# A new order of steps and engines from batch 6's attention on, and two operands' places swapped

## The chip, the cores and the metric

The kernel runs on one core of a Trainium2 chip. The metric is the device time of one execution in microseconds (us). Five engines work side by side, each through its own instructions in order: TensorE (PE, matrix products), VectorE (DVE), ScalarE (ACT), GpSimd (POOL), and SyncE (SP), which starts DMA transfers. They wait for one another through semaphores.

## What is computed

Attention of 8 batches with 8 heads and 576 queries of width 64, whose keys and values are means of 8 neighbours (72 of each), and then a two-layer network over the 4608 resulting tokens of width 512:

```python
k_p = k.reshape(B, H, Sp, pool, D).mean(axis=3)
v_p = v.reshape(B, H, Sp, pool, D).mean(axis=3)
scores = scale * np.matmul(q, k_p.transpose(0, 1, 3, 2))
scores = scores - np.max(scores, axis=-1, keepdims=True)
attn = np.exp(scores)
attn = attn / (np.sum(attn, axis=-1, keepdims=True) + 1e-09)
x = np.matmul(attn, v_p) ...          # (4608, 512)
h = x @ w_in                           # (512, 2048)
g = h * (1.0 / (1.0 + np.exp(-1.702 * h)))
out = g @ w_out                        # (2048, 512)
```

All is fp32. A product of two fp32 operands is made on PE from their high and low parts: each operand is split by a cast (the high part, on ACT or DVE) and a difference (the low part, on POOL or DVE), and three products are summed in a PSUM bank. That is why one entry of a product shows as three or six matmuls.

## The kernel before

The batches are worked one after the other. While PE computes the network of batch c, the other engines and a part of PE prepare the attention of batch c + 1. The last stage handles 1024 tokens at once: the 512 of batch 7 and 8 x 64 that the earlier batches left over.

The width 2048 is cut into 8 pairs p of 256. In the products with w_in a scheme of seven products in place of eight (as Strassen's, in Winograd's form) is used: operands "11" and "21" are quarters of x itself, "22", "t1", "t2", "t3" and "t4" are the last quarter and sums of quarters. For batch 6 these operands lie in `x6` and `xs6_2`, `xs6_3`, ..., its products with w_in go to the banks ha6_p and hb6_p (L1882), and its products with w_out to o6_0, o6_128, o6_256 and o6_384 (L2086 to L2088, three matmuls per pair of parts, here called an o-triple). What ACT and DVE make of a bank before an o-triple is ghall and glall, the high and low part of the gelu, in buffers of the rings `gh` and `gl`.

The 1024-token stage has these steps:

- The late operands: `late_split` and `late_combine` (L1508 to L1548) make y11, y21, y22, yt1 to yt4 from the quarters xtl. `late_op` (L1478) says where they lie; three of them take places of batch 6's operands, so they can be written only when batch 6's last product has read there.
- `hidden(p)` (L2136): seven products of six 512-column matmuls: "11", s2, s3 and "22" into the bank la_p, "12" into lb_p, s1 and s4 into lc_p (L2154). ACT or DVE copies the bank away (`keep`, L2166), DVE adds the other bank (`plus`, L2171), ACT applies the gelu (L2179). A later product into la_p waits for the copy.
- `fold_out(p)` (L2210): sums of w_out's pair, u (L2221, L2232), split into tf (L2237, L2240) in buffers of the rings `gh`, `gl` and `osb`, and written to memory (td, L2253). `fetch_sums` reads them back (ta, tb).
- `operands(th, p)` (L2297): for either half th of the tokens, the operands oa, ob, oc, od with the sums ou, out of the gelus (L2322, L2325, L2331). `outgoing` (L2364): seven products m1 to m7 per pair and half, 112 of six 256-column matmuls (L2376). `combined(th)` adds their banks up (L2404, L2409) and writes the rows out.

Each step is a task of a plan with an engine. The order is written out: `ORDER` is a text of 4738 tokens such as `P:la7_0#0`, whose letter is the engine (A ACT, V DVE, G POOL, P PE, D a DMA on SP's queue, O a writing of rows), and a star moves the task to its other engine: a copy from ACT to DVE, a sum or difference from POOL to DVE. Every engine executes its own tasks in this order, so a task that waits holds all that stands behind it on its engine.

Of the kernel before, what the change touches and what calls it, by code (L numbers as in the profile page):

```python
# [372 lines left out]
A:at7_0#0 A:at7_0#1 V:qt7_1#2 P:ha6_3#1 P:o6_256#5 *A:cs6_3#1 P:o6_128#4 V:nm7_1#0 V:nm7_1#1 A:gh6_3#0 P:o6_128#5
A:cs6_3#2 V:sc7_1#0 P:o6_384#4 G:gl6_3#0 V:qt7_1#3 P:ha6_3#2 V:sc7_1#1 D:ws6_5#1 V:at7_0#0 P:sps7_1#1 A:cs6_3#3
V:cs6_3#1 V:at7_0#1 P:o6_0#6 A:gh6_3#2 V:mt7_0#0 A:cs6_3#6 P:ha6_3#3 *A:ah7_0#0 V:nm7_1#2 G:gl6_3#2 D:ws6_5#3
P:hb6_3#2 V:al7_0#0 A:cs6_3#4 A:gh6_3#1 V:mt7_0#1 P:hb6_4#0 D:ws6_5#2 A:cs6_3#5 V:cs6_3#2 P:hb6_4#1 A:ah7_0#1
V:sc7_1#2 G:gl6_3#1 P:ha6_4#0 V:nm7_1#3 V:al7_0#1 D:ws6_6#0 P:pav7_0#0 V:sc7_1#3 P:o6_384#5 A:xtl0_0#0 *A:cs6_4#0
P:pav7_0#1 A:sc7_1#0 V:mt7_0#2 P:o6_0#7 V:cs6_4#0 *A:ah7_0#2 P:ha6_4#1 V:al7_0#2 A:xtl0_0#1 V:mt7_0#3 P:o6_256#6
A:y1_0#0 V:sm7_1#0 G:xtl0_0#0 A:cs6_4#1 P:o6_128#6 A:gh6_3#3 P:o6_384#6 A:gh6_4#0 A:cs6_3#7 G:xtl0_1#0 P:ha6_4#2
*A:y1_1#0 A:cs6_4#2 V:y1_0#0 A:ah7_0#3 D:ws6_6#1 V:y1_1#0 P:pav7_0#2 A:yt1_0#0 G:gl6_3#3 *A:cs6_4#3 P:o6_128#7  # L380
A:y1_0#1 V:cs6_4#1 G:gl6_4#0 P:ha6_4#3 A:xtl0_0#2 V:al7_0#3 A:gh6_4#2 V:sm7_1#1 G:yt1_0#0 D:ws6_6#3 P:o6_256#7
A:cs6_4#6 V:y1_0#1 A:cs6_4#4 P:hb6_4#2 G:gl6_4#2 A:gh6_4#1 A:cs6_4#5 D:ws6_6#2 P:pav7_0#3 V:cs6_4#2 P:o6_0#8
# [15 lines left out]
P:ha6_7#2 A:gh6_6#1 G:yt3_1#0 *A:yt3_1#1 *G:yt3_0#1 A:cs6_6#5 D:ws7_1#1 P:o6_384#11 *A:cs6_7#3 G:yt3_1#1 A:gh6_6#3
P:o6_128#12 A:cs6_6#7 G:gl6_6#1 P:ha6_7#3 A:gh6_7#0 *G:gl6_6#3 A:cs6_7#2 D:ws7_1#3 P:o6_256#12 *A:y2_0#0 A:y2_0#1
*G:gl6_7#0 A:cs6_7#4 P:o6_0#13 G:y2_0#0 P:o6_384#12 G:y2_0#1 V:cs6_7#1 P:o6_128#13 A:gh6_7#1 P:la7_0#0 A:cs6_7#5  # L400
A:gh6_7#2 *G:gl6_7#1 A:cs6_7#6 P:o6_256#13 *G:gl6_7#2 P:lb7_0#0 D:ws7_2#0 P:o6_384#13 P:o6_0#14 P:hb6_7#2 D:ws7_1#2
A:y2_1#0 *A:y2_1#1 P:lc7_0#0 V:cs6_7#2 G:y2_1#1 *G:y2_1#0 A:gh6_7#3 *G:xtl1_1#1 P:o6_0#15 G:xtl0_2#0 A:cs6_7#7
P:la7_1#0 A:osb6_0#0 *A:yt2_0#1 *A:yt2_1#1 G:xtl0_0#1 *G:xtl1_0#1 A:yt2_0#0 P:o6_256#14 O:osb6_0#0 *A:yt2_1#0
*G:yt2_0#1 A:yt4_0#1 P:o6_128#14 G:yt2_0#0 *G:yt2_1#0 A:yt4_1#1 *G:yt2_1#1 A:yt4_0#0 P:o6_384#14 G:gl6_7#3
*A:yt4_1#0 *G:yt4_0#1 G:yt4_0#0 *G:yt4_1#0 A:store0_0#0 P:o6_256#15 *G:yt4_1#1 G:u1_0#0 A:store1_0#0 *G:u1_1#0
P:o6_128#15 A:osb6_256#0 V:store0_0#0 P:la7_0#1 G:u0#0 A:osb6_128#0 O:osb6_256#0 *G:u0#1 P:lb7_1#0 *A:store0_1#0
A:store0_0#1 G:u0#2 O:osb6_128#0 *A:tf0_0#0 D:ws7_3#0 P:la7_0#2 G:u0#3 V:store1_0#0 A:tf0_2#0 G:tf0_1#0 *G:tf0_2#0
A:w#33 P:la7_1#1 D:ws7_2#1 A:store1_0#1 *A:store0_1#1 G:w#33 V:store0_1#0 P:la7_0#3 G:u1_2#0 A:store1_1#0 *G:u1_3#0
D:td0_0#0 A:store0_1#2 D:td0_0#1 P:lc7_0#1 *G:u1#0 A:store0_0#2 D:ws7_2#3 A:store0_0#3 *G:u1#1 D:td0_1#0 P:lc7_1#0
A:ob0_0#0 V:store0_1#1 G:u1#2 A:tf1_0#0 D:ws7_2#2 *G:ob0_0#0 G:u1#3 A:store0_1#3 P:o6_384#15 *A:tf1_2#0 *G:tf1_1#0  # L410
G:tf1_2#0 P:la7_1#2 A:w#34 D:td1_0#0 A:osb6_384#0 *G:w#34 D:td1_0#1 *G:u1_4#0 G:u1_5#0 P:la7_2#0 D:ws7_3#1
A:store1_1#1 O:osb6_384#0 *G:u2#0 V:store1_1#0 P:lb7_2#0 G:u2#1 A:store2_0#0 D:td1_1#0 A:store1_1#2 *G:u2#2
D:ws7_4#0 P:la7_1#3 *A:tf2_0#0 A:tf2_2#0 G:u2#3 V:store2_0#0 G:tf2_1#0 *G:tf2_2#0 P:lc7_1#1 A:w#35 D:ws7_3#3
*A:store1_0#2 A:store2_0#1 D:td2_0#0 *G:w#35 A:store1_0#3 P:la7_2#1 *G:u1_6#0 G:u1_7#0 D:ws7_3#2 V:store1_1#1
P:lc7_2#0 G:u3#0 A:store2_1#0 D:td2_0#1 *G:u3#1 A:store1_1#3 D:td2_1#0 P:la7_2#2 *A:tf3_0#0 G:u3#2 D:td3_0#0
*G:tf3_1#0 G:u3#3 A:tf3_2#0 P:la7_3#0 *A:store2_1#1 D:ws7_4#1 G:tf3_2#0 A:w#36 V:store2_1#0 P:lb7_3#0 G:w#36
A:store3_0#0 D:td3_0#1 *G:u1_8#0 G:u1_9#0 A:store2_1#2 D:td3_1#0 P:la7_2#3 V:store3_0#0 D:ws7_5#0 G:u4#0
# [2072 lines left out]
```

## Time and profile before

| | us |
|---|---|
| median of three runs | 902.42 |
| lowest and highest run | 901.66 and 902.71 |
| profiled execution | 900.38 |
| its span | 898.6 |

The profiled execution is one of its own, 2.04 us below the median; 1.8 us of it lie outside the span. Times of rows count from the span's start. Busy times of PE come from pipelined matmuls whose ends are modelled, so a start-to-start distance tells more than a length.

### The profile page before, as it was taken

To read this page: it belongs to the slowest core of one execution; us is meant where nothing else is said; L and a number is where in the kernel's file an instruction comes from. 1 tells how busy PE (TensorE), PEld (TensorE's weight loads), DVE (VectorE), ACT (ScalarE), POOL (GpSimd) and SP (SyncE) were. 2 spreads that over 40 slices of the span, in tenths; PEclk is the share of its full clock that TensorE was granted. 3 is DMA by queue.
4 is the path that set the end of the run, shared out by engine and by line. 5 is a ranking of instruction groups with operands and counts; after the bars stand their busy time and mean duration, and the time that the engine had idled before them with its cause. 6 is when DMAs were issued, how large, how long until landed. Compare 5 with 4: busy or idle time off the path is not lost.

```text
span 898.6 us, 15882 instructions
## 1 busy us (share of the span) xinstructions
PE 874.0 (97%) x5404; PEld 780.6 (87%) x5404; DVE 716.8 (80%) x1342; ACT 541.5 (60%) x1188; POOL 387.1 (43%) x377
## 2 busy tenths in 40 slices
...
DMA packets 145793, 174.33 MB, mean 194 GB/s; under 512 B 85169, under 2 KB 96433, under 8 KB 145713
## 3 DMA queue, kind: packets, MB, share of 16 engines
...
## 4 chain that ended last, share of the span: by engine, by line
PE 82%; DVE 4%; POOL 3%; issue 3%; ACT 3%; SPq 2%; DMA 2%; DVEq 0%; POOLq 0%; ACTq 0%
PE ha L1882 13%; PE hb L1882 10%; PE m L2376 9%; PE o L2086 8%; PE o L2087 8%; PE o L2088 8%; PE sps L1128 4%; PE h L1677 3%; PE h L1678 3%; PE h L1679 3%; PE o L1719 2%; PE o L1720 2%; PE o L1721 2%; PE la L2154 2%; POOL u L2221 1%
## 5 line engine op out<-in xcount | busy, mean ns | idle before, releaser
L1936 POOL TENSOR_TENSOR glall<-shared,ghall 128x256 fp32r<-128x256 f32 x80 | 62.8, 790 | 187.5 <-ACT shared L1929 138.9
L2086 PE MATMUL o<-w,ghall 128*128 128x512 f32 x320 | 126.9, 397 | 0.0
L2087 PE MATMUL o<-w,ghall 128*128 128x512 f32 x320 | 126.1, 394 | 0.0
L2088 PE MATMUL o<-w,glall 128*128 128x512 f32 x320 | 125.0, 391 | 0.7 <-POOL glall L1936 0.7
L2088 PEld LDWEIGHTS o<-w,glall 128*128 128x128 f32 x320 | 60.1, 188 | 14.6 <-POOL glall L1936 1.1
L1936 POOL TENSOR_TENSOR glall<-gall,ghall 128x256 fp32r<-128x256 f32 x45 | 34.9, 779 | 87.6 <-ACT gall L1929 51.5
L1882 PE MATMUL ha<-xs,ws 128*128 128x256 f32 x480 | 70.9, 283 | 0.0
L1882 PEld LDWEIGHTS ha<-xs,ws 128*128 128x128 f32 x480 | 66.0, 190 | 4.9 <-ACT shared L1897 0.8
L1882 PE MATMUL hb<-x,ws 128*128 128x256 f32 x480 | 67.2, 283 | 0.0
L2086 PEld LDWEIGHTS o<-w,ghall 128*128 128x128 f32 x320 | 60.6, 189 | 6.2
L1921 ACT ACTIVATE ghall<-shared 128x256 fp32r<-128x256 f32 x108 | 43.9, 415 | 36.6 <-PE o L2087 16.2
L1882 PEld LDWEIGHTS hb<-x,ws 128*128 128x128 f32 x480 | 63.4, 190 | 2.7 <-DVE shared L1904 0.2
L2087 PEld LDWEIGHTS o<-w,ghall 128*128 128x128 f32 x320 | 60.7, 190 | 5.6
L1677 PE MATMUL h<-x,w 128*128 128x256 f32 (+1 forms) x192 | 63.2, 329 | 1.4 <-ACT gh L1699 1.0
L1678 PE MATMUL h<-x,w 128*128 128x256 f32 (+1 forms) x192 | 61.1, 318 | 0.0
L1679 PE MATMUL h<-x,w 128*128 128x256 f32 (+1 forms) x192 | 61.1, 318 | 0.0
L1707 POOL TENSOR_TENSOR gl<-g,gh 128x512 fp32r<-128x512 f32 x28 | 40.0, 1427 | 47.6 <-ACT gh L1699 34.9
L1904 DVE TENSOR_TENSOR shared<-shared,hb 128x256 f32<-128x256 f32 x81 | 33.5, 415 | 22.6 <-PE hb L1882 18.0
L1243 ACT COPY main<-sc 32x256 f32<-32x256 f32 (+2 forms) x109 | 48.5, 445 | 2.9 <-DVE sc L1200 1.1
L1128 PE MATMUL sps<-k,qt 128*128 128x144 f32 x320 | 45.9, 287 | 1.7 <-ACT k L1035 0.7
L1128 PEld LDWEIGHTS sps<-k,qt 128*128 128x128 f32 x320 | 42.7, 190 | 4.1 <-ACT k L1035 1.1
L1929 ACT ACTIVATE shared<-shared 128x256 f32<-128x256 f32 x108 | 43.4, 414 | 3.6 <-ACT osb L1658 0.9
...
## 6 DMA issues: line engine op xcount, KB each, us to landing
...
```

The lines of the kernel that those rows point to most:

```text
L1128: nc.tensor.matmul(ps()[:, t * PW : (t + 1) * PW], lhsT=qt()[:, s0 : s0 + P], rhs=m.k2()[:, jj], start=True, stop=True,)
L1243: copy(out=main()[32 * r : 32 * (r + 1), :, cols].rearrange("p j t (k a) -> p t j a k", a=2), in_=sc()[rows, ts, :, 16 * r : 16 * (r + 1)] ...
L1677: nc.tensor.matmul(o, lhsT=w[:, 0, j], rhs=xs[:, 0], start=j == 0, stop=False)
L1678: nc.tensor.matmul(o, lhsT=w[:, 1, j], rhs=xs[:, 0], start=False, stop=False)
L1679: nc.tensor.matmul(o, lhsT=w[:, 0, j], rhs=xs[:, 1], start=False, stop=j == NJ - 1)
L1882: nc.tensor.matmul(o, lhsT=wv()[:, r, jj], rhs=xo(k, jj), start=start and n == 0, stop=n == len(terms) - 1,  skip_group_check=not start,)
L1921: lambda: nc.scalar.activation(out=gh(), in_=src(), func=AF.Gelu_apprx_sigmoid),
L1936: engine.tensor_tensor(out=gl(), in0=part(i), in1=gh().bitcast(F32), op=ALU.subtract)
L2086: nc.tensor.matmul(o(), lhsT=gh()[:, tok], rhs=w()[:, 0], start=start, stop=False)
L2087: nc.tensor.matmul(o(), lhsT=gh()[:, tok], rhs=w()[:, 1], start=False, stop=False)
L2088: nc.tensor.matmul(o(), lhsT=gl()[:, tok], rhs=w()[:, 0], start=False, stop=stop)
L2376: nc.tensor.matmul(bank()[:, i], lhsT=av(r)[:, i * P : (i + 1) * P], rhs=tv(k), start=p == 0 and i == n == 0, stop=p == NPAIR - 1 and n == ...
```

## The change

`ORDER` is the same up to token 3722. The 1016 tokens behind it, from batch 6's attention part to the end, are the same steps in another order, some of them with the star set or taken away. Of the 1024-token stage, the products lb7_1, la7_0, la7_1 and lb7_0, which take "11" and "21", come first, between o-triples of batch 6; la7_2 and lb7_3 stand with the next ones. Two lines of it, and the two edits beside it:

```diff
-*G:gl6_7#0 A:cs6_7#4 P:o6_0#13 G:y2_0#0 P:o6_384#12 G:y2_0#1 V:cs6_7#1 P:o6_128#13 A:gh6_7#1 P:la7_0#0 A:cs6_7#5
...
+*G:xtl1_1#1 A:gh6_7#3 P:la7_1#0 D:ws7_1#2 A:cs6_7#7 *G:yt2_1#0 A:yt4_0#0 G:yt4_1#0 *G:yt1_1#1 A:yt2_1#1 A:yt3_0#1
...
-            for i, (n, k) in zip(X_PLACES[0], (("t4", 1), ("22", 1), ("t3", 1))):
+            for i, (n, k) in zip(X_PLACES[0], (("22", 1), ("t4", 1), ("t3", 1))):
                 late_ops[n, k] = home(2 * i, [P, 2, CHUNK], F32R, f"y{n}_{k}")
...
-        ha = buf(ps_h, [P, CHUNK], F32, "h", f"la{p}")
-        hb = buf(ps_a, [P, CHUNK], F32, "a", f"lb{p}")
+        ahead = p == 2
+        ha = buf(ps_o if ahead else ps_h, [P, CHUNK], F32, "o" if ahead else "h", f"la{p}")
+        hb = buf(ps_o if ahead else ps_a, [P, CHUNK], F32, "o" if ahead else "a", f"lb{p}")
```

`X_PLACES[0]` is (2, 3, 4). Batch 6 has xs6_2 in place 2 and xs6_3 in place 3; so y22_1 goes from xs6_3's place to xs6_2's, and yt4_1 the other way. The banks la7_2 and lb7_2 come out of the group of banks that held batch 6's o.

The engines of the steps, counted over the whole program (the line numbers are of before, those of after are one lower up to `hidden`):

| steps | DVE | POOL | ACT |
|---|---|---|---|
| late splits and sums (L1516, L1523), before | 18 | 10 | 12 |
| after | 17 | 4 | 19 |
| fold (L2221 to L2240), before | 41 | 38 | 17 |
| after | 40 | 38 | 18 |
| outgoing operands (L2322, L2325, L2331), before | 93 | 42 | 57 |
| after | 112 | 26 | 54 |
| closing sums (L2409), before and after | 14 | 0 | 0 |

PE at the end of batch 6, before: the product hb6_7 that reads xs6_3, between o-triples and the first products of the late stage (la0 and so on are la7_0).

```order
L2086 MATMUL o6_0_7645<-w1_14_1529,ghall0_2959 128x512
L2087 MATMUL o6_0_7645<-w1_14_1529,ghall0_2959 128x512
L2088 MATMUL o6_0_7645<-w1_14_1529,glall0_2977 128x512
L1882 MATMUL hb6_7_8535<-xs6_3_7427,ws6_7_2_8368 128x256 x6
L2154 MATMUL lc0_8661<-yt1_0_8180,ws7_0_1_8423 128x512 x3
L2154 MATMUL lc0_8661<-yt1_1_8491,ws7_0_1_8423 128x512 x3
L2086 MATMUL o6_0_7645<-w1_15_1593,ghall0_2959 128x512
L2087 MATMUL o6_0_7645<-w1_15_1593,ghall0_2959 128x512
L2088 MATMUL o6_0_7645<-w1_15_1593,glall0_2977 128x512
L2154 MATMUL la1_8678<-y11_0_8144,ws7_1_0_8546 128x512 x3
L2154 MATMUL la1_8678<-y11_1_8166,ws7_1_0_8546 128x512 x3
```

After:

```order
L2154 MATMUL lb1_8595<-y21_0_8261,ws7_1_0_8579 128x512 x3
L2154 MATMUL lb1_8595<-y21_1_8331,ws7_1_0_8579 128x512 x3
L2085 MATMUL o6_384_7746<-w1_13_1366,ghall1_3010 128x512
L2086 MATMUL o6_384_7746<-w1_13_1366,ghall1_3010 128x512
L2087 MATMUL o6_384_7746<-w1_13_1366,glall1_3093 128x512
L1881 MATMUL hb6_7_8516<-xs6_3_7427,ws6_7_2_8297 128x256 x6
L2085 MATMUL o6_256_7716<-w1_13_1366,ghall1_3010 128x512
L2086 MATMUL o6_256_7716<-w1_13_1366,ghall1_3010 128x512
L2087 MATMUL o6_256_7716<-w1_13_1366,glall1_3093 128x512
L2085 MATMUL o6_128_7733<-w1_13_1366,ghall0_2959 128x512
L2086 MATMUL o6_128_7733<-w1_13_1366,ghall0_2959 128x512
L2087 MATMUL o6_128_7733<-w1_13_1366,glall0_2977 128x512
```

The product on xs6_3 stands 17 rows earlier, behind a first product lb1 and ahead of la0; the last product that reads xs6_2, whose place y22_1 now takes, stands 24 rows ahead of it.

PE at the last reading of ghall1 and glall1, before:

```order
L2154 MATMUL la0_8620<-yt4_0_8700,shared8_2728 128x512 x3
L2154 MATMUL la0_8620<-yt4_1_8707,shared8_2728 128x512 x3
L2154 MATMUL lc0_8661<-y22_0_8602,ws7_0_2_8509 128x512 x3
L2154 MATMUL lc0_8661<-y22_1_8658,ws7_0_2_8509 128x512 x3
L2154 MATMUL lc1_8820<-yt1_0_8180,ws7_1_1_8576 128x512 x3
L2154 MATMUL lc1_8820<-yt1_1_8491,ws7_1_1_8576 128x512 x3
L2086 MATMUL o6_384_7746<-w1_14_1529,ghall1_3010 128x512
L2087 MATMUL o6_384_7746<-w1_14_1529,ghall1_3010 128x512
L2088 MATMUL o6_384_7746<-w1_14_1529,glall1_3093 128x512
L2154 MATMUL la1_8678<-yt3_0_8554,ws7_1_1_8576 128x512 x3
L2154 MATMUL la1_8678<-yt3_1_8556,ws7_1_1_8576 128x512 x3
```

After:

```order
L2085 MATMUL o6_384_7746<-w1_14_1529,ghall1_3010 128x512
L2086 MATMUL o6_384_7746<-w1_14_1529,ghall1_3010 128x512
L2087 MATMUL o6_384_7746<-w1_14_1529,glall1_3093 128x512
L2154 MATMUL la1_8658<-yt3_0_8541,ws7_1_1_8691 128x512 x3
L2154 MATMUL la1_8658<-yt3_1_8501,ws7_1_1_8691 128x512 x3
L2085 MATMUL o6_256_7716<-w1_14_1529,ghall1_3010 128x512
L2086 MATMUL o6_256_7716<-w1_14_1529,ghall1_3010 128x512
L2087 MATMUL o6_256_7716<-w1_14_1529,glall1_3093 128x512
L2154 MATMUL lc0_8752<-y22_0_8577,ws7_0_2_8571 128x512 x3
L2154 MATMUL lc0_8752<-y22_1_8543,ws7_0_2_8571 128x512 x3
L2154 MATMUL la0_8639<-yt4_0_8669,shared8_2728 128x512 x3
L2154 MATMUL la0_8639<-yt4_1_8628,shared8_2728 128x512 x3
```

POOL at the first fold, whose tf0_1 takes the buffer of ghall1, before:

```order
L1523 TENSOR_TENSOR yt2_0_8688<-xtl0_2_7958,yt2_0_8688 128x256
L1936 TENSOR_TENSOR glall1_3093<-shared12_2925,ghall1_3010 128x256
L1523 TENSOR_TENSOR yt4_0_8700<-xtl0_0_8113,yt4_0_8700 128x256
L2221 TENSOR_TENSOR u0_8730<-w1_0_363 128x512
L2232 TENSOR_TENSOR u0_8730<-u0_8730 128x256 x3
L2240 TENSOR_TENSOR tf0_1_8778<-u0_8730,tf0_0_8764 128x512
L2240 TENSOR_TENSOR w1_0_363<-u0_8730,w1_0_363 128x256
L2221 TENSOR_TENSOR u1_8800<-w1_2_526 128x512
```

After:

```order
L1458 TENSOR_TENSOR xtl0_0_8156<-xtl0_0_8156,xtl0_2_8200 128x512
L1522 TENSOR_TENSOR yt4_1_8628<-xtl0_0_8156,yt4_1_8628 128x256
L1522 TENSOR_TENSOR yt2_1_8651<-xtl1_1_7908,yt2_1_8651 128x256
L2232 TENSOR_TENSOR u0_8702<-u0_8702 128x256 x3
L2240 TENSOR_TENSOR tf0_1_8773<-u0_8702,tf0_0_8771 128x512
L2232 TENSOR_TENSOR u0_8702<-u0_8702 128x256
L2232 TENSOR_TENSOR u1_8793<-u1_8793 128x256 x3
L2240 TENSOR_TENSOR tf1_1_8843<-u1_8793,tf1_0_8819 128x512
L2240 TENSOR_TENSOR w1_2_526<-u1_8793,w1_2_526 128x256
```

The last reading of ghall1 stands behind nine products of the late stage in place of eleven. On POOL tf0_1 is still the first low part, but w1_0's difference is no longer behind it, and one sum of the next pair follows.

DVE at the end, the closing sums of the second half, before:

```order
L2409 TENSOR_TENSOR store0_1_8760<-store0_1_8760,m6_1_9989 128x512
L2409 TENSOR_TENSOR store1_1_8802<-store0_1_8760,m7_1_9978 128x512
L2409 TENSOR_TENSOR store0_1_8760<-store0_1_8760,m5_1_9967 128x512
L2409 TENSOR_TENSOR store3_1_9035<-store1_1_8802,m5_1_9967 128x2x256
L2409 TENSOR_TENSOR store3_1_9035<-store1_1_8802,m4_1_9955 128x2x256
L2409 TENSOR_TENSOR store2_1_8937<-store0_1_8760,m3_1_9997 128x2x256
L2409 TENSOR_TENSOR store2_1_8937<-store0_1_8760,m2_1_9944 128x2x256
```

After:

```order
L2409 TENSOR_TENSOR store2_1_8909<-store0_1_8733,m2_1_9906 128x2x256
L2409 TENSOR_TENSOR store0_1_8733<-store0_1_8733,m6_1_9961 128x512
L2409 TENSOR_TENSOR store1_1_8766<-store0_1_8733,m7_1_9971 128x512
L2409 TENSOR_TENSOR store3_1_8956<-store1_1_8766,m4_1_10004 128x2x256
L2409 TENSOR_TENSOR store3_1_8956<-store1_1_8766,m5_1_9946 128x2x256
L2409 TENSOR_TENSOR store0_1_8733<-store0_1_8733,m5_1_9946 128x512
L2409 TENSOR_TENSOR store2_1_8909<-store0_1_8733,m3_1_9996 128x2x256
```

PE's last five products are m7, m5, m4, m3, m2 before, and m7, m4, m5, m3, m3 after. Before, the sum of m2 is the last and that of m3 the one ahead; now the sum of m2 stands first and that of m3 last.

## Rows read from the trace of the kernel before

**Rows 1.** The page's first part and its chain, whole span: busy, share

```profile
span 898.6 us, 15882 instructions
...
PE 874.0 (97%) x5404; PEld 780.6 (87%) x5404; DVE 716.8 (80%) x1342; ACT 541.5 (60%) x1188; POOL 387.1 (43%) x377
...
PE 82%; DVE 4%; POOL 3%; issue 3%; ACT 3%; SPq 2%; DMA 2%; DVEq 0%; POOLq 0%; ACTq 0%
```

**Rows 2.** Times of PE's waits from 600 us on: engine, line, releaser: total, times, longest

```profile
PE la L2154 <- ACT store L2166: 4.3, 3, 3.4
PE lb L2154 <- DVE store L2171: 2.5, 1, 2.5
...
PE pav L1367 <- DVE y L1418: 1.1, 2, 0.7
PE o L2088 <- POOL glall L1936: 0.7, 1, 0.7
PE lc L2154 <- DVE store L2171: 0.7, 1, 0.7
```

**Rows 3.** Timeline of PE, 728 to 790 us: start, length, instructions, idle before in brackets

```profile
729.43 2.61 PE L2154 MATMUL la<-yt,ws 128*128 128x512 f32 x6 [3.43 <-ACT store L2166]
...
739.33 1.52 PE L2154 MATMUL lc<-yt,ws 128*128 128x512 f32 x6
740.69 0.39 PE L2086 MATMUL o<-w,ghall 128*128 128x512 f32 x1
...
746.80 2.86 PE L2154 MATMUL lb<-y,ws 128*128 128x512 f32 x6 [2.54 <-DVE store L2171]
749.90 1.83 PE L2154 MATMUL la<-yt,shared 128*128 128x512 f32 x6 [0.24 <-ACT store L2166]
752.40 1.66 PE L2154 MATMUL lc<-y,ws 128*128 128x512 f32 x6 [0.67 <-DVE store L2171]
...
761.16 1.66 PE L2154 MATMUL la<-yt,shared 128*128 128x512 f32 x6 [0.31 <-DVE store L2166]
...
769.11 1.65 PE L2154 MATMUL la<-yt,ws 128*128 128x512 f32 x6 [0.85 <-DVE store L2166]
...
787.88 1.67 PE L2154 MATMUL la<-yt,ws 128*128 128x512 f32 x6 [0.65 <-ACT store L2166]
```

**Rows 4.** Times of the waits of all engines, 714 to 747 us

```profile
POOL tf L2240 <- PE o L2087: 9.2, 1, 9.2
POOL y L1523 <- DVE y L1516: 6.7, 1, 6.7
DVE u L2221 <- POOL w L2240: 6.5, 1, 6.5
...
ACT store L2166 <- POOL u L2232: 4.3, 1, 4.3
...
DVE y L1516 <- PE hb L1882: 3.5, 1, 3.5
```

**Rows 5.** Busy times in two windows, columns as headed in the page: granted clock third last

```profile
730.00:750.00 20.00, 17.21 (x63) 13.10 (x62) 9.30 (x17) 8.50 (x17) 8.21 (x9) 0.84 0.56 182
808.47:893.00 84.53, 83.53 (x685) 82.83 (x683) 71.87 (x101) 33.36 (x60) 42.81 (x37) 1.00 0.16 54
```

**Rows 6.** Times of the waits of SP's queue, 700 to 815 us

```profile
SPq L2253 <- POOL tf L2240: 10.4, 4, 6.4
```

**Rows 7.** Groups by form, DVE, 820 to 880 us: busy, mean ns, idle before

```profile
L2325 DVE TENSOR_TENSOR ob<-store,ob 128x256 fp32r<-128x256 f32 x13 | 12.5, 964 | 0.0
L2325 DVE TENSOR_TENSOR od<-ou,od 128x512 fp32r<-128x512 f32 x13 | 10.8, 830 | 0.9 <-ACT od L2322 0.9
...
L2331 DVE TENSOR_TENSOR ou<-store 128x256 f32<-128x256 f32 x12 | 6.1, 512 | 0.3
```

**Rows 8.** Timeline at the end, 886 to 899 us

```profile
888.51 4.66 DVE L2409 TENSOR_TENSOR store<-store,m 128x512 f32<-128x512 f32 x7 [8.12 <-PE m L2376]
...
890.40 0.88 PE L2376 MATMUL m<-w,od 128*128 128x256 f32 x6
...
891.12 0.88 PE L2376 MATMUL m<-w,oa 128*128 128x256 f32 x6
```

More of the change, by code (lines that the diff above doesn't have):

```diff
@@ L373 @@
[L373 to L382, printed above, removed]
@@ L398 @@
[L398 to L407, printed above, removed]
@@ L408 @@
[L408 to L417, printed above, removed]
@@ new lines @@
+V:y1_1#0 *A:cs6_5#1 A:main7_1#0 P:pav7_0#2 *A:main7_1#15 P:ha6_5#2 V:cs6_5#0 *A:tail7_1#7 *A:y1_0#1 A:cs6_5#3
+G:gl6_4#2 A:main7_1#2 *A:main7_1#7 P:o6_0#8 A:tail7_1#2 P:o6_384#8 A:tail7_1#1 *A:tail7_1#0 A:main7_1#5 V:cs6_5#1
+V:y1_0#0 D:xtl1_1#1 A:cs6_4#7 V:al7_0#3 A:main7_1#4 P:hb6_5#2 P:ha6_5#3 V:cs6_5#2 D:ws6_7#2 A:main7_1#6 D:ws6_7#1
+G:gl6_4#3 P:o6_256#8 D:ws6_6#1 *A:tail7_1#6 P:o6_256#9 G:xtl0_0#0 A:tail7_1#4 A:gh6_5#2 P:ha6_6#0 A:gh6_5#0
+*G:gl6_4#1 P:pav7_0#3 A:main7_1#9 A:cs6_5#2 A:y1_1#1 *A:main7_1#14 D:ws6_7#3 P:o6_384#9 *A:cs6_6#0 G:gl6_5#0
@@ new lines @@
+A:y2_0#0 D:ws7_1#0 V:y1_0#3 *G:gl6_6#3 V:cs6_7#0 *G:gl6_6#2 P:o6_0#12 A:xtl1_1#2 *G:xtl1_1#0 A:y2_1#1 *G:y2_0#0
+P:o6_0#13 P:lb7_1#0 *G:xtl0_2#0 A:gh6_7#0 A:cs6_7#4 A:yt2_0#0 A:cs6_7#2 A:yt1_1#1 P:o6_384#12 P:hb6_7#2 *A:y2_0#1
+*G:gl6_7#0 P:o6_256#12 G:xtl0_0#1 A:gh6_7#2 P:o6_128#13 A:yt4_1#0 P:o6_384#13 A:gh6_7#1 *G:y2_1#1 A:cs6_7#6
+*G:gl6_7#2 D:ws7_1#3 *G:yt2_0#0 P:la7_0#0 P:o6_256#13 A:yt3_1#1 V:cs6_7#2 A:yt2_1#0 *G:y2_0#1 A:cs6_7#5 A:xtl1_0#3
+*G:xtl1_1#1 A:gh6_7#3 P:la7_1#0 D:ws7_1#2 A:cs6_7#7 *G:yt2_1#0 A:yt4_0#0 G:yt4_1#0 *G:yt1_1#1 A:yt2_1#1 A:yt3_0#1
@@ new lines @@
+*G:yt3_0#1 P:lb7_0#0 A:yt2_0#1 *G:gl6_7#1 P:o6_256#14 P:o6_128#14 D:ws7_1#1 *G:yt2_0#1 D:ws7_0#3 P:o6_0#14
+*G:yt4_0#0 *G:gl6_7#3 *G:yt3_1#1 G:yt2_1#1 *G:u1_0#0 A:store0_0#0 *G:xtl1_0#1 D:ws7_3#0 A:yt4_0#1 *A:store1_0#0
+P:o6_0#15 A:yt1_0#1 P:la7_0#1 *G:yt1_0#1 *G:u1_1#0 V:store1_0#0 P:o6_384#14 A:store0_1#0 G:u0#0 A:yt4_1#1 A:osb6_0#0
+P:la7_1#1 P:la7_0#2 P:lc7_0#0 G:u0#1 P:o6_128#15 G:u0#2 D:ws7_2#0 A:store1_1#0 P:o6_384#15 *A:tf0_0#0 G:tf0_1#0
+A:store0_1#1 P:la7_1#2 D:td0_0#0 V:store0_0#0 *G:yt4_1#1 A:tf0_2#0 G:u0#3 *G:tf0_2#0 A:w#33 V:store0_1#0 *G:yt4_0#1
@@ new lines @@
+O:osb6_0#0 *G:w#33 *G:u1_2#0 G:u1#0 A:osb6_128#0 *G:u1_3#0 *A:store1_1#1 P:o6_256#15 D:td0_1#0 *G:u1#1 O:osb6_128#0
+P:lc7_0#1 G:u1#2 G:u1#3 A:osb6_256#0 D:ws7_2#2 A:tf1_0#0 A:store1_0#1 P:la7_0#3 D:td0_0#1 P:lc7_1#0 P:la7_2#0
+G:tf1_1#0 V:store1_1#0 A:w#34 G:w#34 A:store0_0#2 A:tf1_2#0 G:tf1_2#0 *A:store2_0#0 P:la7_1#3 V:store0_1#1 D:ws7_3#1
+D:ws7_2#1 A:store0_0#3 *G:u1_4#0 A:store1_0#2 P:lc7_1#1 D:td1_0#1 A:store0_0#1 P:lb7_3#0 *G:u1_5#0 G:u2#0 G:u2#1
+A:tf2_0#0 D:ws7_2#3 V:store1_1#1 P:la7_2#1 O:osb6_256#0 D:ws7_3#2 G:u2#2 *G:u2#3 D:ws7_3#3 P:la7_3#0 A:store2_1#0
@@ new lines @@
+P:lb7_2#0 *G:tf2_1#0 *A:tf2_2#0 G:tf2_2#0 A:w#35 D:td2_1#0 *A:store3_0#0 P:la7_2#2 G:w#35 D:td1_0#0 G:u1_6#0 G:u3#0
+P:lc7_2#0 *G:u1_7#0 *A:store2_1#1 *G:u3#1 G:u3#2 V:store2_1#0 P:la7_3#1 A:store3_1#0 D:ws7_4#0 P:la7_2#3 *G:u3#3
+A:tf3_2#0 A:store0_1#2 V:store3_0#0 A:tf3_0#0 *G:tf3_1#0 P:lc7_2#1 A:w#36 V:store2_1#1 G:tf3_2#0 P:lb7_4#0 G:w#36
+P:la7_3#2 D:ws7_5#0 *G:u1_9#0 D:td2_0#1 A:store3_1#1 D:ws7_4#1 P:la7_4#0 *G:u1_8#0 P:lc7_3#0 *G:u4#0 P:la7_3#3
+D:ws7_4#2 D:td3_1#0 D:td3_0#0 D:td3_0#1 A:osb6_384#0 *A:store4_0#0 G:u4#1 *G:u4#2 *G:u4#3 A:w#37 *A:tf4_0#0
@@ new lines @@
+V:store4_0#0 V:store3_1#0 P:la7_4#1 D:td2_0#0 D:ws7_5#1 *A:ob0_0#0 *G:tf4_1#0 O:osb6_384#0 G:w#37 A:tf4_2#0
+A:store4_1#0 P:lc7_3#1 A:store3_0#2 P:la7_4#2 *G:tf4_2#0 *G:ob0_0#0 D:ws7_4#3 G:u1_10#0 V:store3_1#1 P:la7_5#0
+P:lc7_4#0 D:td1_1#0 *G:u1_11#0 *G:u5#0 A:store4_1#1 G:u5#1 D:td4_0#0 P:lb7_5#0 D:ws7_5#2 *A:store5_0#0 *G:u5#2
+A:tf5_2#0 *G:u5#3 *G:tf5_2#0 A:tf5_0#0 G:tf5_1#0 V:store4_1#0 D:ws7_6#0 A:w#38 P:la7_4#3 G:w#38 A:store4_1#2
+*G:u1_13#0 P:lc7_4#1 *G:u1_12#0 D:ws7_5#3 V:store4_1#1 G:u6#0 G:u6#1 A:store4_0#2 P:la7_5#1 G:u6#2 A:tf6_0#0
```

131 lines of the change are left out of this document (65 added, 66 removed).

## The prediction

> **What bounds the kernel now.** I read the page first: TensorE (PE) is busy for 97% of the 898.6 us, and the chain of work that ended last runs through it for 82% [rows 1]. So the time is the time of PE's instructions plus PE's pauses, and an edit that leaves every product in place can give back only pauses. The times of PE's own waits come second: from 600 us on, three sorts of them hold most: 4.3 us on `ACT store L2166`, 2.5 us on `DVE store L2171`, 0.7 us on `POOL glall` [rows 2]. They are no lack of engine time but of places, as the timeline shows where they lie: a pause of 3.43 us ahead of the product at 729.43, one of 2.54 us at 746.80, and five of 0.24 to 0.85 us up to 787.88 [rows 3]. The waits of all engines from 714 to 747 us name what stood behind the two long ones [rows 4].
>
> First pause. VectorE (DVE) waited 3.5 us to write the operand y22, POOL 6.7 us for what DVE writes there, and the releaser of DVE's wait is `PE hb L1882`, the last product of batch 6 on xs6_3, whose place y22_1 takes [rows 4]. Behind it the engines had all the rest of the late splits to do at once, ACT's next copy of a product bank waited another 4.3 us [rows 4], and PE stood at 729.43. Second pause. POOL's tf0_1 (the low part of the first folded w_out pair) waited 9.2 us for `PE o L2087`, the last o-product that reads a gelu buffer of the same ring; DVE's next u stood 6.5 us behind POOL [rows 4]. That o-product is the one at 740.69 [rows 3]. The fold's work then came in a lump ahead of the store that lb7_2 needed at 746.80.
>
> The products in that stretch also run long, and the granted clock of 730 to 750 us is 0.84, with 17.21 us of PE work in 20 [rows 5]; before it PE had stood for 3.43 us. A product of six 512-column matmuls takes 1.36 us from start to start at best (739.33 to 740.69), but the seven from 729.43 to 740.69 took 11.26 us where 7 x 1.36 = 9.52, so 1.74 too much; the product at 746.80 shows 2.86 us against 1.52, so 1.34 too much; the ones at 749.90 and 752.40 another 0.31 and 0.14 [rows 3]. Together 3.53 us of slow clock.
>
> **The change part by part.**
>
> *Place of y22_1.* It now takes the place of xs6_2, whose last reader stands 24 rows of PE's order ahead of the product on xs6_3; that product itself stands 17 rows earlier. Two reasons, either of which suffices, take away the wait for y22. What is late next is the splits themselves: the sets t1 to t4 and 22, made by three engines. The four products lb7_1, la7_0, la7_1, lb7_0 use only "11" and "21", which need no sums of quarters, and stand between o-triples, so the splits of t2, t3 and t4 get the time of those products as cover (two more full products than before, 2.7 us) on top of the 3.5 us that DVE idled. 6.2 us of cover against a pause of 3.43 and the 0.7 ahead of `POOL glall` [rows 2, 3]: I take both at nothing, 4.13 us gained. From below: if the splits fill that cover to the brim, a late start like the 0.65 to 0.85 us of [rows 3] stays.
>
> *Release of tf0_1.* The last read of its buffer now stands behind nine late products instead of eleven, and no 3.43 us pause lies ahead of it. Worked from 741.37: less 3.43, less 0.7, less 2 x 1.36, less 1.74 of slow clock makes about 732.8. POOL comes to tf0_1 about when it did, so its wait of 9.2 us shrinks to 1 us or less, and the fold starts some 8.5 us earlier while PE at this point is 4.1 + 1.7 + 2.7 = 8.5 us ahead by the same sum, 2.7 of it only by order. Against PE's need it is 2.7 us earlier, and the pause was 2.54. That is tight, but lb7_2 is no longer what comes next either: it moves behind lb7_3, with banks of its own for la7_2 and lb7_2 (`ps_o`). I take the 2.54 us as gone; kept whole at the other end.
>
> *Slow clock.* It followed the two long pauses. With them gone I take all 3.53 us back; at the other end, a single long pause that stays keeps about half.
>
> *The later pairs.* The five small pauses from 749.90 to 787.88 sum to 0.24 + 0.67 + 0.31 + 0.85 + 0.65 = 2.72 us [rows 3]. The new order is as dense, its starts rest on the same stores, and I see no reason for another size: they count as unchanged, with 0 to 6 us as bounds, since each of seven pairs can lose as much as the largest, 0.85.
>
> *Weights and folds on SP's queue.* SP starts the loads of weights and the writes of folded sums in one order. It stood 10.4 us in four waits for `POOL tf`, the longest 6.4 [rows 6]. With tf0_1 early, the longest goes. The traffic itself is unchanged. Nothing taken.
>
> *Engines of the last stage.* In the building of the outgoing operands 112 instructions stand on DVE instead of 93, and 26 on POOL instead of 42; with the 14 closing sums DVE has 126. Its rows from 808.47 to the end are 101 for 71.87 us, 0.71 each, while POOL was busy for 42.81 [rows 5]. DVE works there beside POOL and slows: the 256-column differences that split ob take 964 ns, the first sums of ou, as wide, 512 [rows 7]; the closing sums, 512 columns wide and with POOL idle, take 4.66/7 = 0.67 us [rows 8]. 126 x 0.71 = 89.5 us is the upper bound, by this stage's own mean; with half of the instructions of either width at 0.51 and 0.67, 126 x 0.59 = 74 us is the lower one. The cover is 112 outgoing products on PE, 0.72 us from start to start [rows 8], some 80 us, and some 10 us of the last pairs beside which the first operands are already built: 90 us. Both ends fit, so I take nothing; beyond 0.71 each 0.01 costs 1.26 us.
>
> *Tail.* The last two products now both go to the bank of one sum, and the sums on the other banks stand ahead. Before, seven sums ran 4.66 us from 888.51 to 893.17 while PE's last products ended at 892.0 [rows 8], so 1.17 us behind PE. After, one sum of 0.68 us is left: 0.5 us gained (0 to 0.5).
>
> *Attention of batch 6.* Its steps are in another order with other engines too. Of PE's pauses there the list shows 1.1 us in two, for `y` [rows 2]. I take no change, with 1.5 us either way, which is two or three waits of that size more or less.
>
> **Sum.** The profiled execution took 900.38 us. 900.38 - 4.13 - 2.54 - 3.53 - 0.5 = 889.7. The median of the runs is 902.42, 2.04 us above the profiled one, so the forecast is 889.7 + 2.0 = 891.7 us. With the small terms at their bounds it lies between 886.7 (small pauses gone, 1.5 better in the attention, and 0.76 less for the lowest run in place of the median) and 896.5 (3.3 more in the pairs, 1.5 in the attention).
>
> **The rivals.**
>
> *Half comes back.* The pauses move on: PE now reaches pairs 2 to 4 some 10 us sooner, and must find their weights and stores there. For it: SP's queue is served in order and held for 10.4 us in waits on folds [rows 6]; against it: the fold's engines stand idle in 730 to 750, DVE with 9.30 us and POOL with 8.21 of 20 [rows 5]. Half of 10.2 us stays lost: 891.7 + 5.1 = 896.8 us.
>
> *The wait was not what it seemed.* If DVE's, ACT's and POOL's splits alone fill the time to 728, with or without the wait for y22, PE only stands elsewhere. For it: PE's pause ended with `ACT store`, itself behind POOL's u, and not with y22 [rows 2, 4]. Against it: DVE and POOL idled at once. Time: 902.4 less the 0.5 of the tail, 902 us.
>
> *DVE becomes the bound of the last stage,* and the kernel gets slower. If the 19 added instructions meet POOL's remaining ones as badly as the split ob and od do, 964 and 830 ns [rows 7], and the mean comes to 0.85, DVE needs 126 x 0.85 = 107 us for a cover of 90: 17 us late, 908.7 us. It decides from a mean of 0.80 on: (90 + 10.7)/126, where the whole gain is eaten. For it: 71.87 busy us of 84.53 already [rows 5]. Against it: with 16 fewer instructions POOL meets DVE less often.
>
> *Each microsecond of POOL stops DVE for one.* Then DVE's 74 us and POOL's 26/42 x 42.81 = 26.5 us [rows 5] add up to 100.5, 10.5 more than the cover, and the time is 902.2 us: no change. Against it: before, the same sum is 107 x 0.59 + 42.81 = 106 us, where DVE's row has 71.87 and the list of PE's waits has none for an outgoing product [rows 2, 5]. The Trainium skill (SBUF — State Buffer, "Who interferes with whom") states this as a rule: a DVE instruction with two SBUF inputs and a GpSimd instruction that reads SBUF exclude each other, and the one that starts second stands until the first ends. By that rule, the trace agrees in direction, 964 ns against 512 [rows 7], and not in size.
>
> **How the numbers follow.** Forecast 0.57; half 0.20; not what it seemed 0.08; POOL's time added to DVE's 0.04; DVE the bound 0.11. A measurement of this kernel tells about 0.2%, 1.8 us, from no change. Forecast and half are faster by more: 0.77. The third and the fourth lie within: 0.12. DVE the bound is slower: 0.11. The range reaches from 886.5 over the forecast and over half, whose own upper end is near 901 by the same bounds as the forecast's: 886.5 to 901. What is left out, 902 and more, has 0.2 or a little over.
>
> **What would show it.** Right: no pause of PE over 1 us from 714 to 760, first products of la7_0 on t2 at 1.5 us, a granted clock near 1 in that stretch, tf0_1 at 731 to 734, the first outgoing product near 799 instead of 808.5, and DVE's rows behind it at 0.71 us or less with no wait of `PE m`. Wrong: PE waiting for `od`, `oc` or `oa` in the last stage, or a pause over 2 us on `ws` or `store` in pairs 2 to 4.

## The result and the profile after

The changed kernel takes 894.2 us (median of four runs, 892.25 to 894.7) where the kernel before, on the same chip, takes 902.57: a ratio of 0.9904 with a 95% interval of 0.9887 to 0.9921. The forecast was 891.7 in a range of 886.5 to 901. Of the 8.4 us the two traces can show 5.9, from 898.6 to 892.7 us of span: the traced execution of before, 900.38 us, is 2.2 under its median, that of after, 894.48, within 0.3 of its own.

The page of after, its first part and its chain, as in [rows 1]:

```profile
span 892.7 us, 15828 instructions
...
PE 872.2 (98%) x5404; PEld 781.6 (88%) x5404; DVE 698.4 (78%) x1376; ACT 538.0 (60%) x1186; POOL 343.6 (38%) x345
...
PE 87%; DMA 3%; DVE 3%; ACT 2%; SPq 1%; issue 1%; POOL 1%; DVEq 0%; POOLq 0%; ACTq 0%
```

PE is busy for 1.8 us less; the rest of the 5.9 is pauses. The times of PE's waits from 600 us on, as in [rows 2] (engine, line, releaser, total, times, longest):

```profile
PE la L2154 <- ACT store L2166: 5.9, 1, 5.9
PE lc L2154 <- DVE store L2171: 0.5, 1, 0.5
```

The ten waits of before are down to two, but the one on `ACT store` is longer than any before. PE's timeline shows where both lie, as in [rows 3] (start, length, instructions, idle before in brackets):

```profile
750.46 1.52 PE L2154 MATMUL la<-yt,shared 128*128 128x512 f32 x6
752.51 1.66 PE L2154 MATMUL lc<-y,ws 128*128 128x512 f32 x6 [0.53 <-DVE store L2171]
...
769.63 2.93 PE L2154 MATMUL la<-yt,ws 128*128 128x512 f32 x6 [5.90 <-ACT store L2166]
772.36 1.99 PE L2154 MATMUL la<-y,ws 128*128 128x512 f32 x6
774.18 1.53 PE L2154 MATMUL lc<-yt,ws 128*128 128x512 f32 x6
775.56 1.52 PE L2154 MATMUL lb<-y,ws 128*128 128x512 f32 x6
```

From 690 us to 752 PE has no pause at all; the pauses at 729.43 and 746.80 of [rows 3] are gone. At 769.63 stands a new one of 5.90 us, and the products behind it run long: 2.73 us from 769.63 to 772.36, 1.82 to 774.18 and 1.38 to 775.56, where 1.36 is the step, so 1.85 us too much. The windows show the granted clock (third column from the right, 1.00 is full speed), then the last stage, as in [rows 5]:

```profile
720.00:740.00 20.00, 20.00 (x90) 16.54 (x89) 12.57 (x26) 7.12 (x16) 7.51 (x10) 1.00 0.51 170
760.00:780.00 20.00, 14.10 (x55) 11.20 (x54) 9.09 (x18) 5.42 (x11) 4.86 (x6) 0.83 0.59 203
802.76:887.03 84.27, 83.55 (x685) 82.83 (x683) 66.85 (x125) 38.42 (x74) 26.19 (x26) 1.00 0.20 75
```

So the slow clock moved with the pause, from 0.84 in 730 to 750 us [rows 5] to 0.83 in 760 to 780. The chain of the stretch ahead of the new pause, in order of time (start, us, what), names its cause:

```profile
754.61 5.79 DMA td<-tf
...
760.49 0.59 ACT osb L1657
...
761.10 7.57 DMA out_dram<-osb
...
768.69 0.40 ACT tf L2237
769.10 0.49 ACT store L2166
...
769.63 2.50 PE la L2154 x5
```

and the waits of all engines there show what stood still with it:

```profile
POOL u L2221 <- DVE tf L2240: 7.0, 1, 7.0
ACT tf L2237 <- DMA out_dram<-osb: 6.8, 1, 6.8
...
DVE tf L2240 <- ACT tf L2237: 6.3, 2, 5.9
...
PE la L2154 <- ACT store L2166: 5.9, 1, 5.9
...
ACT osb L1657 <- DMA td<-tf: 2.9, 1, 2.9
```

Read the chain from its end: PE waits for ACT's copy of a bank (769.10), the copy stands behind the cast tf4_2 (768.69), and that cast waits for a transfer of 7.57 us that began at 761.10. It writes the last rows of batch 6, osb6_384, out of a buffer that tf4_2 takes next: both come from the ring `osb`, which has two. In the kernel before, the writing of osb6_384 began at 748.9. In the new order its copy stands behind pair 3's part of the fold that has the other buffer of this ring: it waits 2.9 us for that part's transfer (754.61, 5.79 us) and starts at 760.49, right ahead of pair 4's tf4_2.

The end, as in [rows 8]:

```profile
882.75 4.28 DVE L2409 TENSOR_TENSOR store<-store,m 128x512 f32<-128x512 f32 x6 [0.68 <-PE m L2376]
...
884.71 1.60 PE L2376 MATMUL m<-w,od 128*128 128x256 f32 x12
```

DVE's last sum ends 0.72 us behind PE's products (887.03 against 886.31), before 1.17. The groups of DVE's forms in the middle of the last stage, as in [rows 7] (busy, mean ns, idle before):

```profile
L2325 DVE TENSOR_TENSOR od<-ou,od 128x512 fp32r<-128x512 f32 x11 | 8.0, 724 | 0.8 <-ACT od L2322 0.8
...
L2325 DVE TENSOR_TENSOR ob<-store,ob 128x256 fp32r<-128x256 f32 x9 | 3.8, 444 | 0.0
...
L2331 DVE TENSOR_TENSOR ou<-store 128x256 f32<-128x256 f32 x19 | 7.9, 448 | 0.1
```

The split of ob takes 444 ns there where it took 964 (605 over the whole stage), and DVE's 125 rows of this stage 66.85 us where 101 took 71.87 [rows 5, 7].

### The profile page after: what moved, and what is told of

The parts are those of the page before. It is cut to its first block, busy times and chain, and to the rows that moved or that the text cites. A ratio compares the mean times of both kernels' runs of the same rounds, so it can differ in the third digit from the quotient of the medians.

```text
span 892.7 us, 15828 instructions
## 1 busy us (share of the span) xinstructions
PE 872.2 (98%) x5404; PEld 781.6 (88%) x5404; DVE 698.4 (78%) x1376; ACT 538.0 (60%) x1186; POOL 343.6 (38%) x345
## 4 chain that ended last, share of the span: by engine, by line
PE 87%; DMA 3%; DVE 3%; ACT 2%; SPq 1%; issue 1%; POOL 1%; DVEq 0%; POOLq 0%; ACTq 0%
PE ha L1881 13%; PE hb L1881 10%; PE m L2376 9%; PE o L2085 8%; PE o L2086 8%; PE o L2087 8%; PE sps L1127 4%; PE la L2154 3%; PE h L1676 3%; PE h L1677 3%; PE h L1678 3%; PE o L1718 2%; PE o L1719 2%; PE o L1720 2%; PE lc L2154 2%
## 5 line engine op out<-in xcount | busy, mean ns | idle before, releaser
L1935 POOL TENSOR_TENSOR glall<-shared,ghall 128x256 fp32r<-128x256 f32 x76 | 60.0, 794 | 203.4 <-ACT shared L1928 149.9
L1935 POOL TENSOR_TENSOR glall<-gall,ghall 128x256 fp32r<-128x256 f32 x42 | 32.4, 775 | 84.0 <-ACT gall L1928 51.8
```

Source lines behind the costliest of these rows:

```text
L1935: engine.tensor_tensor(out=gl(), in0=part(i), in1=gh().bitcast(F32), op=ALU.subtract)
```

## The experiments

In each kernel the order's text is wrapped anew, so its line numbers differ by a few.

**The new pause: osb6_384 earlier.** In the kernel after, two tokens move.

```diff
 A:w#34
+A:osb6_384#0 O:osb6_384#0
 G:w#34
...
 D:td3_0#1
-A:osb6_384#0
 *A:store4_0#0
...
 *G:tf4_1#0
-O:osb6_384#0
 G:w#37
```

> The kernel after, with one step moved: the copy of batch 6's last bank o6_384 (osb6_384) and the writing of its rows stand on ACT right behind w#34 (about 740 us) and no longer ahead of tf4_2 (760.5 us). Theory A (the one pause left, 5.90 us at 769.63, comes from a ring of two buffers: tf4_2 takes the buffer of osb6_384 and waits 7.6 us for the transfer of its rows, and ACT's copy store4_1 stands behind it): the pause and the slow clock behind it (1.85 us) go, the time falls by 6 to 8 us against the kernel after, to 886 to 888.5 us. Theory B (the late fold itself, POOL and DVE, is what holds pair 4): the pause moves to another wait, and the time stays within 2 us of the kernel after's 894.

Measured: 887.86 us (887.11 to 889.37), 0.9845 of before with an interval of 0.9830 to 0.9859. PE's waits from 600 us on are now

```profile
PE la L2148 <- ACT store L2160: 0.8, 1, 0.8
PE lc L2148 <- DVE store L2165: 0.5, 1, 0.5
PE hb L1875 <- DMA ws<-wd: 0.5, 1, 0.5
```

The pause of 5.90 us is gone and nothing of its size took its place; by the two ratios to before, 0.9845 and 0.9904, it is 5.3 us ahead of the kernel after, by the medians 6.3. That is theory A, if the ratios put the gain a little under the 6 to 8 us it named, and a kernel that beats both.

**The same wait, passed by ACT alone.** In the kernel after, ACT's copy goes ahead of the waiting cast; the transfer stays where it is.

```diff
 G:w#37
+A:store4_1#0
 A:tf4_2#0
-A:store4_1#0
 P:lc7_3#1
```

> The kernel after with one exchange on ACT: the copy store4_1, on which PE's product at 769.63 waits, stands ahead of tf4_2, the fold's cast that waits for the transfer of batch 6's last rows. The transfer and its wait stay. Theory A (the cost lies only in ACT's order): the pause of 5.90 us goes, 6 to 8 us are gained, 886.5 to 888.5 us, as with the earlier osb6_384. Theory B (DVE has the same wait in its order: tf4_2's low part stands ahead of store3_1, whose bank PE needs two products later): the product at 769.63 starts at once, and PE waits 3 to 4.5 us some three products later for a DVE store; 1.5 to 3 us are gained, 891 to 892.5 us.

Measured: 893.58 us (889.92 to 895.44), 0.9914 of before (0.9894 to 0.9934). PE's pause, and the waits behind it:

```profile
768.07 1.66 PE L2148 MATMUL la<-y,ws 128*128 128x512 f32 x6 [3.61 <-ACT store L2160]
```

```profile
POOL u L2215 <- DVE tf L2234: 6.2, 1, 6.2
DVE tf L2234 <- ACT tf L2231: 5.5, 2, 5.0
ACT tf L2231 <- DMA out_dram<-osb: 4.8, 1, 4.8
```

Neither theory as written: the product of 769.63 starts on time, but the very next one waits 3.61 us, and not for DVE but for another of ACT's copies, which still stands behind the cast. This traced execution is the fastest of the four, and its transfer holds the cast for 4.8 us where it was 6.8. The interval overlaps that of the kernel after, so a gain isn't shown. Letting one instruction pass the wait only handed it to the next; with the wait itself away, in the run ahead of this one, the gain is there.

**The first long pause: the places alone.** In the kernel before, only the places of y22_1 and yt4_1 are exchanged.

```diff
-            for i, (n, k) in zip(X_PLACES[0], (("t4", 1), ("22", 1), ("t3", 1))):
+            for i, (n, k) in zip(X_PLACES[0], (("22", 1), ("t4", 1), ("t3", 1))):
```

> The kernel before, with only the places of y22_1 and yt4_1 exchanged. Theory A (the wait for y22's place makes the first long pause): DVE's wait of 3.5 us and POOL's of 6.7 us for y22 go, the 3.43 us pause at 729.43 falls under 1 us, and with the slow clock behind it 4 to 6 us are gained: 897 to 899 us. Theory B (the splits fill the time to 728 anyway): the pause stays at 3 us or more, and the time is 902 to 903 us.

Measured: 901.5 us, 0.9991 of before (0.9980 to 1.0002): no difference that this can tell. PE's pause stands where it stood, and so does the wait, in the waits of all engines:

```profile
729.43 2.93 PE L2147 MATMUL la<-yt,ws 128*128 128x512 f32 x6 [3.42 <-ACT store L2159]
...
747.66 2.32 PE L2147 MATMUL lb<-y,ws 128*128 128x512 f32 x6 [2.54 <-DVE store L2164]
```

```profile
POOL xtl L1452 <- DVE y L1516: 3.4, 1, 3.4
...
DVE shared L1897 <- PE hb L1875: 3.3, 1, 3.3
```

DVE no longer waits for y22's place, and waits 3.3 us for the same product of PE all the same: in its order the sum of that product's bank (`shared` out of `hb`) stands ahead of what y22 still needs. The theory of the place falls; the time agrees with theory B, but the wait on hb is there, so B's reason isn't shown by this run; the next one contradicts it.

**The product instead of the place.** In the kernel before, batch 6's last product on xs6_3 moves.

```diff
 P:o6_128#13
+P:hb6_7#2
 A:gh6_7#1
...
 P:o6_0#14
-P:hb6_7#2
 D:ws7_1#2
```

> The kernel before, with only batch 6's last product on xs6_3 (hb6_7) moved ahead of la7_0's first product, some 4.8 us earlier on PE. Theory A (in DVE's order the sum of that product's bank stands ahead of y22's low part, so the product's late place holds DVE, whichever place y22_1 takes): DVE's waits of 3.3 to 3.5 us for hb go, and the 3.43 us pause at 729.43 falls under 1 us; with the slow clock 4 to 6 us are gained, 897 to 899 us, where the exchange of places alone gave 0.9. Theory B (the splits themselves fill the time until ACT's copy at 728.8): the pause stays over 2 us and less than 2 us are gained.

Measured: 896.27 us, 0.9922 of before (0.9901 to 0.9944). PE's timeline:

```profile
728.82 1.64 PE L2147 MATMUL lb<-y,ws 128*128 128x512 f32 x6 [0.29 <-DVE store L2164]
...
743.20 1.66 PE L2147 MATMUL lb<-y,ws 128*128 128x512 f32 x6 [2.54 <-DVE store L2164]
746.28 1.64 PE L2147 MATMUL la<-yt,shared 128*128 128x512 f32 x6 [1.41 <-ACT store L2159]
```

The pause of 3.43 us is down to 0.29, 6.5 us are gained by one token, and the second pause, 2.54 us, is untouched. The waits from 708 to 750 us have none for hb any more. This is theory A, a little more than it said: it was the product's late place that held DVE, ACT and POOL.

**The second long pause: the last o-triple.** In the kernel before:

```diff
 P:o6_256#15
+P:o6_384#15
 *G:yt4_1#1
...
 A:store0_1#3
-P:o6_384#15
 *A:tf1_2#0
```

> The kernel before, with only the last o-triple of o6_384 moved from behind lc7_1 to right behind the last one of o6_256, seven late products earlier. Theory A (POOL's tf0_1 is held by that triple): its wait of 9.2 us falls to 3 us or less, the 2.54 us pause at 746.80 goes, and 2.5 to 5 us are gained: 897.5 to 900 us. Theory B (pair 2's pause comes from the amount of fold work and not from the wait): the pause at 746.80 stays at 2 us or more and the time is 902 us.

Measured: 899.59 us, 0.9964 of before (0.9946 to 0.9981). The pause of 2.54 us ahead of lb7_2 is gone, with POOL's long wait; of its gain a part is given back:

```profile
731.87 1.91 PE L2147 MATMUL la<-yt,ws 128*128 128x512 f32 x6 [2.74 <-ACT store L2159]
...
748.64 1.66 PE L2147 MATMUL la<-yt,shared 128*128 128x512 f32 x6 [1.26 <-ACT store L2159]
...
756.12 1.67 PE L2147 MATMUL la<-yt,ws 128*128 128x512 f32 x6 [1.74 <-ACT store L2159]
```

The pauses of 1.26 and 1.74 us were 0.24 and none in [rows 3]; POOL's waits ahead of its tf are 1.3 us in two where one was 9.2. So the triple did hold POOL, as theory A says. That the earlier fold then meets the next stores in ACT's order is a reading of the releaser's name and not tested. Nor are the 2.8 us between the medians the pause of 2.54 itself: this kernel's runs lie between 896.17 and 902.27, the first pause is 2.74 here in place of 3.43, and the spans of the two traces differ by 0.3 us.

**Pairs of these edits.** The places with the triple, and the product with the triple, both in the kernel before.

> The kernel before with both of the two small edits (places exchanged, last triple of o6_384 earlier) and the rest of the order and all engines as before. If these two waits are what the change gave back, the gains add up: 8 to 10 us, 892.5 to 895 us, the time of the kernel after. If the new engines and the rest of the new order carry a good part, it stays at 897 us or more.

Measured: 898.03 us, 0.9952 of before (0.9937 to 0.9967). With the first pause still at 2.77 us the triple gives its share and no more. The time is that of the second case, 897 or more, but not for its reason, as the next pair shows.

> The kernel before with the product hb6_7 earlier and the last triple of o6_384 earlier; places, engines and the rest of the order as before. If the two late products of batch 6 are what held the 1024-token stage, the time is that of the kernel after or better, 891 to 894.5 us. If the rest of the new order (first products without sums) does its own part, it stays above 896 us.

Measured: 893.36 us, 0.9894 of before (0.9878 to 0.9909), as fast as the kernel after. PE's waits:

```profile
PE la L2147 <- ACT store L2159: 3.9, 3, 1.6
PE pav L1360 <- DVE y L1411: 1.1, 2, 0.7
PE la L2147 <- DVE store L2159: 0.9, 1, 0.9
```

Two tokens of the order of before, with its places, banks and engines, reach the time of the whole change. No pause over 1.64 us is left in them, where the kernel after has one of 5.90 and hardly any other; with that one taken away the whole change is 4.4 us ahead of the two tokens (0.9845 against 0.9894). The ring `osb` is not free of waits here either: one of ACT's tf waits 3.4 us for the transfer of batch 6's rows. What that costs PE was not tried.

**DVE in the last stage: all of POOL's steps on DVE.** In the kernel after, a star for each of POOL's 26 steps there, as in

```diff
-G:oc0_1#0
+*G:oc0_1#0
```

> The kernel after with the 26 sums and differences of the outgoing operands that POOL still has moved to DVE, 152 there in all with the closing sums, none on POOL. Theory A (each microsecond of POOL's work costs DVE most of one; solving 101u + 42.81k = 71.87 of before and 125u + 26.19k = 66.85 of after gives u = 0.35 us and k = 0.86): DVE is busy for about 152 x 0.35 = 53 us behind the first outgoing product, less than with POOL's help, and the time stays at 894 us within 1.5 us since PE did not wait there. Theory B (0.59 us each alone, as the prediction took): 90 us for 84 us of PE's work, PE waits for operands, and the kernel is 4 us or more slower than after.

Measured: 893.62 us, 0.9896 of before (0.9877 to 0.9914), the same as the kernel after. The last stage in one window, and the two commonest forms:

```profile
802.77:887.05 84.28, 83.56 (x685) 82.83 (x683) 70.28 (x150) 38.30 (x74) 0.85 (x1) 1.00 0.20 76
```

```profile
L2326 DVE TENSOR_TENSOR ou<-store 128x256 f32<-128x256 f32 x25 | 9.8, 420 | 0.2
...
L2320 DVE TENSOR_TENSOR od<-ou,od 128x512 fp32r<-128x512 f32 x13 | 8.9, 685 | 0.5 <-ACT od L2317 0.5
```

150 rows take 70.28 us, 0.469 each. The time is theory A's, but both missed the size: 53 us was too low, 90 far too high. PE has no wait in that stage.

**The engines of the last stage alone.** In the kernel before, the stars of the outgoing operands as in the kernel after, 67 tokens, the order as it was: 34 steps go from POOL to DVE and 18 back, 9 from ACT to DVE and 6 back, 19 more on DVE in all.

> The kernel before with only the engines of the outgoing operands set as in the kernel after, the order as before. Theory A: DVE's busy time behind the first outgoing product falls from 71.87 to 64 to 68 us although it executes some 19 instructions more, and the time stays within 0.3% of before, 900 to 904 us, since PE had no pause there. Theory B: DVE, already at 71.87 of 84.53 us, becomes the bound and the kernel is 5 us or more slower than before.

Measured: 902.6 us, 0.9999 of before (0.9989 to 1.0010).

```profile
810.60:895.31 84.71, 83.54 (x685) 82.83 (x683) 62.88 (x116) 31.88 (x57) 25.57 (x25) 1.00 0.15 53
```

116 rows take 62.88 us where 101 took 71.87 [rows 5]: more instructions on DVE in less time, and no change of the kernel's time. Theory A, with the busy time slightly under what it said.

Not tried: the kernel after without the exchange of places, and with la7_2 and lb7_2 in their old banks. Whether the new order could run without either isn't shown here.

## Why the forecast held

**How near it was, and what of that is luck.** By the medians the forecast is 2.5 us off. By the traces, for which its sum was worked out, it is 4.8 us off (889.7 against 894.48), and 5.9 of the 10.7 us came, about what the case "half comes back" gives (5.6). The medians look better because the traced execution of before was faster than its median and that of after wasn't. The two long pauses went by the mechanism that was named; in the small terms 7.75 us were lost from 763 us on and 3.3 gained (2.19 and 1.1), neither of them foreseen, and that the measured time stays near all the same is luck. One of the prediction's own signs of being wrong was seen, a pause over 2 us on `store` in pairs 2 to 4, and the first outgoing product came at 802.76, not near 799.

**First pause, 4.13 us.** Gained in full: no pause over 0.53 us from 690 to 763, where the new one begins. The step's reason failed in one half. It said that either the exchange of places or the product's earlier stand would suffice. The exchange alone took away the wait for y22 but gave nothing that can be told (0.9991), the product alone 6.5 us. That run has none of the four first products as cover either, so the 6.2 us of cover that the prediction counted on are not needed to lose this pause; what they add in the kernel after isn't separated. The order of DVE should have been read one row further: the sum of that same product's bank stands there, between y22's two parts.

**Second pause, 2.54 us.** Gone in full, and right in its mechanism, which the triple's run shows. POOL's tf0_1 ran at 732.74, where 732.8 was worked out from PE's side. What failed is the step that its wait "shrinks to 1 us or less" because POOL comes about when it did: POOL came earlier too and stood for 6.05 us, DVE with the high part for 4.46. The rows of after:

```profile
730.05 0.43 DVE L2237 CAST tf<-u 128x512 fp32r<-128x512 f32 x1 [4.46 <-PE o L2086]
```

```profile
732.74 1.29 POOL L2240 TENSOR_TENSOR tf<-u,tf 128x512 fp32r<-128x512 f32 x1 [6.05 <-DVE yt L1522]
```

The profile names DVE for POOL's wait; PE's last o-triple of o6_256, the last reader of the buffer, starts at 732.04 and is just as near. The wait cost PE nothing, so the error had no price.

**Slow clock, 3.53 us.** Right as a consequence: with the pauses gone the granted clock is 1.00 from 720 to 760. But the slow clock came back with the new pause, 1.85 us, the half that the prediction gave to one long pause. Not every pause brings it: the run with the product alone moved has one of 2.54 us and a clock of 1.00 from 728 to 750, the run with store4_1 ahead one of 3.61 and 1.00 from 750 to 780.

**The later pairs, taken as unchanged.** This is the mis-sized term. The five small pauses of 2.72 us are one of 0.53, a gain of 2.2; against it stands one of 5.90 us with 1.85 of slow clock, outside the bound "as much as the largest, 0.85" for each pair. What failed is the reason that the starts rest on the same stores: the stores are the same, but the order ahead of them on ACT holds a step moved there from elsewhere, the rows of batch 6; that they made the pause is shown by the run that moves them alone. The case "half comes back" had the right size in the trace (its cause was put to SP's queue of weights and folds, and it was ACT's).

**Attention and tail.** The 1.1 us of waits for `y` [rows 2] are gone, taken as unchanged; the tail gave 0.2 in place of 0.5 (PE's last end to the span's end, 6.6 us before and 6.39 after): DVE's last sum is 0.45 us nearer to PE's end, as forecast, and the writing behind it takes 0.24 longer.

**The sum of the traces.** 4.13 + 2.54 + 3.53 + 2.19 + 1.1 + 0.2 = 13.7 us gained, 5.90 + 1.85 = 7.75 lost, 5.9 left, which is the difference of the spans.

**DVE in the last stage, taken as nothing.** Right, and with more room than the sum gave. The lower bound of 0.59 us an instruction was too high: with POOL silent it is 0.469, with 420 and 685 ns for the two widths. The 512 ns row that stood for "alone" was itself beside POOL's work. The rival in which DVE binds the stage from 0.80 us on had its sign wrong: moving steps from POOL made each of DVE's shorter, 0.535 us with 26 of POOL's left and 0.71 with 37. The other rival, one microsecond of DVE for each of POOL's, would need 58.6 + 26.2 = 85 us after (125 x 0.469), where the row has 66.85: 0.31 us lost per microsecond of POOL, and before (71.87 - 101 x 0.469)/42.81 = 0.57, a rough figure since the widths are not mixed alike. The Trainium skill's rule of exclusion (SBUF — State Buffer, "Who interferes with whom") agrees with these runs in its direction: with more of POOL's time, 42.81 us against 26.19, DVE's rows are longer, 0.71 us against 0.535. How much of a wait falls on POOL's side no run here shows, as none has POOL alone, so the rule's size stays untested, and the prediction's "not in size" with it.
